# Attention in 64x64 quadrants of TensorE, with the work of two pairs of heads spread over three visits

## The chip, the cores and the metric

One core of a Trainium2 chip runs the whole kernel. The metric is device microseconds (us) of one execution, taken as the median of several executions. TensorE does the matmuls, ScalarE the exponentials, logarithms and sines, VectorE and GpSimd the elementwise work. PSUM, where TensorE writes, is used by this kernel as four "bank pairs" of 2 x 512 float32 per partition.

## The reference

Normalised queries and keys, softmax attention, then two products with an activation between them:

```python
q_n, k_n = rmsnorm(q, g_q), rmsnorm(k, g_k)          # q, k, v: 8 x 12 x 448 x 64
attn = softmax(q_n @ k_n.T / sqrt(64))
x = (attn @ v).transpose(0, 2, 1, 3).reshape(3584, 768)
h = x @ w_in                                          # w_in: 768 x 2048   "first product"
g = h + sin(alpha * h)**2 / (alpha + 1e-9)
out = g @ w_out                                       # w_out: 2048 x 768  "second product"
```

The kernel leaves out the softmax's maximum. It gets the sums of the exponentials by a second matmul against ones beside each value matmul, and multiplies by exp(-ln(sum)).

## The kernel before

A batch has 12 heads, taken as six pairs. Keys come in tiles: three of 128 tokens for one pair, and a rest of 64 tokens that is computed for two pairs at once. So three shapes of the TensorE array alternate: scores in 64\*128 (contraction over 64, 128 outputs), values in 128\*64, the rest in 64\*64.

```python
psum = ctx.enter_context(tc.tile_pool(name="ps", bufs=4, space=bass.MemoryType.PSUM))

def scores(pi, t, warm=0):                     # pair pi, key tile t of 128: mode 64*128
    sc = bank_pair("sc")
    ...
    for hi in range(2):
        r = slice(hi * 64, hi * 64 + 64)
        nc.tensor.matmul(sc[:, hi, :S], kt[r, t * P:(t + 1) * P], qt[r, :], start=True, stop=True)
    nc.scalar.activation(expT[pi][:, 2 * t:2 * t + 2, :], sc[:, :, :S], ACT.Exp, scale=SCALE)

def attend(pi):                                # values and sums: modes 128*64 and 64*64
    av = bank_pair("av")
    for t in range(NT + 1):
        for part in range(2):
            for hi in range(2):
                ...
                nc.tensor.matmul(av[o, part, :S], lhsT, rhs, start=(t == 0), stop=(t == NT))
    rec = rpool.tile([P, S], F32, tag="rec", name="rec")
    nc.scalar.activation(rec, av[:, 1, :S], ACT.Ln)
    nc.scalar.activation(rec, rec, ACT.Exp, scale=-1.0)
    ...
    for hi in range(2):
        nc.vector.tensor_mul(xT[b][r, hp, :], av[r, 0, :S], rec[o, :])
```

A bank pair `av` comes free only after ScalarE's logarithm, ScalarE's exponential, and both VectorE products.

Steps of the previous batch's second product are the fillers. They keep TensorE busy while ScalarE makes exponentials. Each pair of heads is one visit:

```python
for p in range(NP):                            # NP = 6 pairs; for each batch b >= 1
    ...
    scores(pi, 0)
    scores(pi, 1)
    if p:
        attend(pi - 1)
    ...
    if p % 2 == 0:
        rest_scores(pi)                        # 64*64, for pairs pi and pi + 1
    scores(pi, 2)
    beside_e(4 * p)                            # norm of later batches, loads
    fill(...)                                  # some 9 steps of the second product (128*128)
    ...
attend(b * NP + NP - 1)
first_product(b, beside_h(b))
```

Of the kernel before, what the change touches and what calls it, by code (L numbers as in the profile page):

```python
# [32 lines left out]
def kernel(  # L33
# [19 lines left out]

    nc = tc.nc
# [9 lines left out]
    NJ = S // REST  # L64
    NC = NP // 2
    SCALE = float(D) ** -0.5
    HALF = D_MODEL // 2
    BUSY = (20, 8, 0, 8, 4, 4, 4, 4)
# [10 lines left out]
    epool = ctx.enter_context(tc.tile_pool(name="expT", bufs=3))  # L79
# [7 lines left out]
    def bank_pair(name):  # L87
        return psum.tile([P, 2, 512], F32, tag="ps", name=name)
# [11 lines left out]
    def rest_rows(pi, hi):  # L100

        r = (hi + pi) % 2
        return slice(r * 64, r * 64 + 64)

    def load_v(b):


        vb[b] = vpool.tile([P, NT * H + NP, D], BF16, tag="vb", name="vb")
        parts = []
        tok = v[b].rearrange("h (p j) d -> p h (j d)", j=NJ)  # L110
        for jj in range(2):
            parts.append((vb[b][jj * 64:jj * 64 + 64, :NT * H, :].rearrange("p (h t) d -> p h (t d)", t=NT),
                          tok[:, :, jj * NT * D:(jj + 1) * NT * D]))
        last = v[b].rearrange("(hi dp pp) (p j) d -> j hi pp p dp d", hi=2, pp=2, j=NJ)[NJ - 1]
        slots = vb[b][:, NT * H:, :].rearrange("p (dp pp) d -> pp p dp d", pp=2)
        for hi in range(2):
            for pp in range(2):
                parts.append((slots[pp][rest_rows(pp, hi)], last[hi, pp]))
        return [lambda o=o, i=i: nc.gpsimd.dma_start(out=o, in_=i) for o, i in parts]  # L119
# [64 lines left out]
    def norm_tasks(ci):  # L184
# [3 lines left out]

# [29 lines left out]
        def scale(w):  # L218
            eng = nc.vector if early else nc.gpsimd
            if st.n is None:  # L220
                st.n = npool.tile([P, 2, NJ, 2, D], BF16, tag="qkn", name="qkn")
            n, x = st.n[:, w], qk[ci][:, w].rearrange("p (hi j) d -> p hi j d", hi=2)
            inv = st.inv[w].rearrange("p (hi j) -> p hi j", hi=2)
            for hi in range(2):
                if w == 0:
                    eng.tensor_mul(n[:, :, hi, :], x[:, hi], inv[:, hi].unsqueeze(2).to_broadcast([P, NJ, D]))  # L226
                else:
                    eng.tensor_mul(  # L228
                        n[:, :2 * NT, hi, :].rearrange("p (t jj) d -> p jj t d", jj=2),
                        x[:, hi, :2 * NT].rearrange("p (jj t) d -> p jj t d", jj=2),  # L230
                        inv[:, hi, :2 * NT].rearrange("p (jj t) -> p jj t", jj=2).unsqueeze(3).to_broadcast([P, 2, NT, D]))
            if w == 1:
                eng.tensor_mul(n[:, NJ - 1], x[:, :, NJ - 1], inv[:, :, NJ - 1].unsqueeze(2).to_broadcast([P, 2, D]))
# [33 lines left out]
    def scores(pi, t, warm=0):  # L267

        sc = bank_pair("sc")
        for _ in range(warm):  # L270
            nc.tensor.matmul(sc[:, 0], blank[:, :P], blank, start=True, stop=True)
        qt, kt = qkT[pi][:, 0, :], qkT[pi][:, 1, :]
        if pi not in expT:
            expT[pi] = epool.tile([P, 2 * NT + 1, S], BF16, tag="expT", name="expT")
        for hi in range(2):
            r = slice(hi * 64, hi * 64 + 64)
            nc.tensor.matmul(sc[:, hi, :S], kt[r, t * P:(t + 1) * P], qt[r, :], start=True, stop=True)  # L277
        nc.scalar.activation(expT[pi][:, 2 * t:2 * t + 2, :], sc[:, :, :S], ACT.Exp, scale=SCALE)  # L278

    def rest_scores(pi):  # L280

        sc = bank_pair("sc3")
        for pp in range(2):
            if pi + pp not in expT:
                expT[pi + pp] = epool.tile([P, 2 * NT + 1, S], BF16, tag="expT", name="expT")
            for hi in range(2):
                r = slice(hi * 64, hi * 64 + 64)
                nc.tensor.matmul(sc[rest_rows(pp, hi), pp, :S], qkT[pi + pp][r, 1, NT * P:S], qkT[pi + pp][r, 0, :],  # L288
                                 start=True, stop=True)
        for pp in range(2):  # L290
            nc.scalar.activation(expT[pi + pp][:, 2 * NT, :], sc[:, pp, :S], ACT.Exp, scale=SCALE)  # L291

    def attend(pi):
# [3 lines left out]
        e = expT[pi]  # L297
        av = bank_pair("av")
        for t in range(NT + 1):
            for part in range(2):  # L300
                for hi in range(2):
                    o = slice((hi + part) % 2 * 64, (hi + part) % 2 * 64 + 64)
                    if t < NT:
                        lhsT = ones if part else vb[b][:, (hi * NP + hp) * NT + t, :]
                        rhs = e[:, 2 * t + hi, :]
                    else:
                        r = rest_rows(pi, hi)
                        lhsT = ones[r, :] if part else vb[b][r, NT * H + hp, :]
                        rhs = e[r, 2 * NT, :]
                    nc.tensor.matmul(av[o, part, :S], lhsT, rhs, start=(t == 0), stop=(t == NT))  # L310
# [23 lines left out]
    def first_product(b, beside):  # L334
# [11 lines left out]
        for i in range(EARLY):  # L346
            tiles[i] = bank_pair("hps")
            for m in (2 * i, 2 * i + 1):
                mm(tiles[i], m, range(KT - 1))
        for i in range(MT // 2):  # L350
            if i >= EARLY:
                tiles[i] = bank_pair("hps")
            for m in (2 * i, 2 * i + 1):
                mm(tiles[i], m, [KT - 1] if i < EARLY else range(KT))
            for m in (2 * i, 2 * i + 1):
                late.append(snake(b, tiles[i][:, m % 2, :S], m))
                if len(late) > 1:
                    late.popleft()()
            for task in beside.get(i, ()):
                task()  # L360
# [77 lines left out]
    def step_of(ci, *steps):  # L438
        return lambda: [norm[ci].steps[n]() for n in steps]
# [9 lines left out]
    FIRST, KEPT = 16, MT // 2  # L449
    for p in range(NP):  # L450
        scores(p, 0, BUSY[2 + p])
        scores(p, 1)
        if p:
            attend(p - 1)
        if p == 0:
            c1.rsqrt()
        if p % 2 == 0:
            rest_scores(p)
        scores(p, 2)
        if p == 0:  # L460
            c2.square(0), c2.square(1)
            c2.fold_g()
            c1.scale(0), c1.scale(1)
            c2.reduce(0), c2.reduce(1)
            load_qk(NC)
        if p == 1:
            c1.pe_transpose((0, 1))
            c2.rsqrt()
            c2.scale(0), c2.scale(1)
            load_qk(NC + 1)  # L470
            load_w_out(0)
            begin_norm(NC)
            step_of(NC, 0, 1, 2)()
        if p == 2:
            c2.pe_transpose((0, 1))
            step_of(NC, 3, 4)()
            v_parts = load_v(1)
            v_parts[0](), v_parts[1]()
            begin_norm(NC + 1)
            step_of(NC + 1, 0, 1, 2)()  # L480
        if p == 3:
            step_of(NC, 5, 6)()
            step_of(NC + 1, 3, 4)()
            for part in v_parts[2:]:
                part()
            load_w_out(1)
        if p == 5:
            step_of(NC + 1, 5)()
    step_of(NC + 1, 6)()
    attend(NP - 1)  # L490
    first_product(0, beside_h(0))

    for b in range(1, B):
# [20 lines left out]
        def beside_e(slot):  # L514
            for task in at[slot]:
                task()

        for p in range(NP):
            pi = b * NP + p
            if p == 0:  # L520
                quota = min(FIRST, n_fill)
            else:
                left = max(n_fill - FIRST, 0)
                quota = left * p // (NP - 1) - left * (p - 1) // (NP - 1)
            part = [quota * j // 4 for j in range(5)]
            if p == 0 and b > 1:
                fill(part[2])
            scores(pi, 0)
            scores(pi, 1)
            if p:  # L530
                attend(pi - 1)
            else:
                fill(part[3] - (part[2] if b > 1 else 0))
            if p % 2 == 0:
                rest_scores(pi)
            scores(pi, 2)
            beside_e(4 * p)
            if p:
                fill(part[2])
                beside_e(4 * p + 1)  # L540
                fill(part[3] - part[2])
            else:
                beside_e(4 * p + 1)
            beside_e(4 * p + 2)
            fill(part[4] - part[3])
            beside_e(4 * p + 3)
        attend(b * NP + NP - 1)
        for slot in range(4 * NP, len(at)):
            beside_e(slot)
# [31 lines left out]
```

## Time and profile before

| | before |
|---|---|
| time, median of 4 runs | 457.88 us (457.71 to 459.25) |
| TensorE busy | 96% of the span |
| one batch (first product to first product, batches 2 to 7) | 52.47 us |
| ... its 271 matmul slots at their own pace | 48.27 us |
| ... its 33 changes of array mode | 3.70 us |
| ... the rest, which is waits | 0.50 us |
| first product of batch 0 starts | 46.6 us |

The last four lines come from the start of every matmul in the trace. A slot is one matmul, or two or four that run side by side in parts of the array. It takes 189 ns for 448 columns and 162 ns for 384. What a start is late by, where the shape of the array changes, is booked as a mode change, and what is left as a wait. The split is sharper than the waits that the profile lists, because a listed wait counts only from the modelled end of the group before.

The profile's own list of TensorE's waits (columns: total us, times, longest) has these two on top for the whole run:

```profile
PE av L310 <- ACT expT L278: 3.0, 9, 0.9
PE av L310 <- DMA vb<-in_v_dram: 2.2, 1, 2.2
```

The second is one wait of batch 0 for V. No value or score waits for VectorE's product `xT`.

### The profile page before, as it was taken

Reading aid. Unit: us, or ns where it says so; the run is one execution under the profiler, and the core shown is the slowest. Engines: PE = TensorE matmul, PEld = TensorE weight load, DVE = VectorE, ACT = ScalarE, POOL = GpSimd, SP = SyncE. Lnnn points to the kernel's source line nnn. Section 1 sums busy time; section 2 is a strip of 40 time slices with the busy share of each in tenths; the row PEclk is TensorE's granted clock in tenths of the full one; section 3 lists DMA queues with packets and bytes.
Section 4 is the critical chain, followed back from the end, with each engine's and each line's share of the span. In section 5 each row is a group of like instructions: output and inputs, shape, how many; then the busy total and the mean of one; then the engine's idle time right before and its main releaser. Section 6 shows DMA issues by size and latency. Waiting matters only on the chain.

```text
span 456.9 us, 7795 instructions
## 1 busy us (share of the span) xinstructions
PE 436.8 (96%) x2952; PEld 215.0 (47%) x2956; DVE 227.9 (50%) x334; ACT 341.6 (75%) x555; POOL 293.1 (64%) x299
## 2 busy tenths in 40 slices
PE   7678999999999999999999999999999999999996
PEld 3333544445444554445444554445544454445563
DVE  3774374536545465444655364554745364333621
ACT  4869788868888688877888589777888588876700
POOL 3977977777768687686668697686677686002400
PEclk9989999999999999999999999999999999999999
DMA  6999999378055922579064941469043750410022
GB/s 242 185 243 243 219 159 245 94 148 153 2 156 156 142 93 69 113 161 204 0 156 148 98 145 30 128 169 219 1 144 87 69 85 3 97 48 19 0 58 81
DMA packets 81833, 54.98 MB, mean 120 GB/s; under 512 B 60148, under 2 KB 78340, under 8 KB 81796
## 3 DMA queue, kind: packets, MB, share of 16 engines
q1 hardware_dynamic: 56690, 40.97, 35.1%
q0 software_dynamic: 24160, 11.81, 21.1%
q10 hardware_dynamic: 946, 1.70, 1.0%
q8 instruction: 23, 0.38, 0.3%
q14 instruction: 14, 0.11, 0.1%
HBM read 45.62 MB, written 11.01 MB: 124 GB/s over the span
## 4 chain that ended last, share of the span: by engine, by line
PE 81%; ACT 8%; issue 3%; DMA 3%; DVE 2%; POOL 2%; SPq 0%; DVEq 0%; POOLq 0%
PE hps L341 32%; PE ops L383 26%; PE av L310 16%; PE sc L277 6%; ACT expT L278 4%; DMA vb<-in_v_dram 2%; ACT expT L291 2%; DVE ms L208 1%; POOL s L325 1%; DMA g_rows<-in_g_q_dram 1%; ACT rec L313 1%; ACT rec L312 1%; PE sc L288 1%; ACT inv L215 1%; DVE g_sb L330 0%
## 5 line engine op out<-in xcount | busy, mean ns | idle before, releaser
L383 PE MATMUL ops<-w_out_sb,g_sb 128*128 128x384 bf16 x896 | 155.6, 327 | 1.9 <-DVE g_sb L330 1.0
L341 PE MATMUL hps<-xT,w_in_sb 128*128 128x448 bf16 x768 | 146.7, 353 | 0.0
L278 ACT ACTIVATE expT<-sc 128x896 bf16<-128x896 f32 x144 | 125.6, 916 | 25.5 <-PE sc L277 25.3
L383 PEld LDWEIGHTS <-g_sb 128*128 128x128 bf16 x896 | 83.6, 98 | 65.3 <-issue 13.1
L330 DVE SCALAR_TENSOR_TENSOR g_sb<-s,inv_alpha_sb,hps 128x448 bf16<-128x448 f32 x128 | 81.2, 676 | 63.3 <-POOL s L325 63.3
L325 POOL TENSOR_TENSOR s<-s 128x448 f32<-128x448 f32 x64 | 59.3, 930 | 76.1 <-ACT s L322 64.2
L318 DVE TENSOR_TENSOR xT<-av,rec 64x448 bf16<-64x448 f32 x96 | 59.7, 622 | 96.5 <-ACT rec L313 94.6
L341 PEld LDWEIGHTS <-w_in_sb 128*128 128x128 bf16 x768 | 74.5, 98 | 70.3 <-issue 1.6
L322 ACT ACTIVATE s<-hps,alpha_sb 128x448 f32<-128x448 f32 x128 | 74.5, 627 | 28.5 <-PE hps L341 26.8
L310 PE MATMUL av<-expT,vb 128*64 128x448 bf16 (+1 forms) x384 | 71.2, 364 | 5.2 <-ACT expT L278 3.0
L202 POOL TENSOR_TENSOR sq<-qk 128x896 f32<-128x896 f32 x42 | 69.9, 1678 | 5.9 <-DVE ms L208 3.2
L226 POOL TENSOR_TENSOR qkn<-qk,inv 128x448 bf16<-128x448 f32 x42 | 38.5, 937 | 50.4 <-issue 33.2
L310 PE MATMUL av<-expT,ones 128*64 128x448 bf16 (+1 forms) x384 | 67.1, 358 | 0.0
L205 POOL TENSOR_TENSOR qk<-qk,gg 128x896 f32<-128x896 f32 x24 | 50.1, 2090 | 3.7 <-ACT gg L155 3.3
L388 DVE COPY osb<-ops 128x768 f32<-128x768 f32 (+1 forms) x35 | 27.9, 797 | 45.5 <-PE ops L383 45.4
L208 DVE TENSOR_REDUCE ms<-sq 128x14 f32<-128x896 f32 x42 | 44.8, 1081 | 9.8 <-POOL sq L202 9.6
L277 PE MATMUL sc<-qkT 64*128 64x448 bf16 x288 | 44.7, 359 | 2.0 <-ACT expT L291 0.6
L310 PEld LDWEIGHTS <-vb 128*64 128x64 bf16 (+1 forms) x384 | 22.8, 108 | 46.5 <-issue 39.4
L312 ACT ACTIVATE rec<-av 128x448 f32<-128x448 f32 x48 | 26.1, 544 | 21.7 <-PE av L310 19.5
L327 ACT ACTIVATE s<-s 128x448 f32<-128x448 f32 x64 | 36.9, 577 | 2.9
L228 POOL TENSOR_TENSOR qkn<-qk,inv 128x384 bf16<-128x384 f32 x42 | 33.9, 828 | 0.0
L119 POOL DMA_DIRECT2D vb<-in_v_dram x48 | 32.1, 686 | 0.0
(50 smaller groups left out, 196.2 us busy)
## 6 DMA issues: line engine op xcount, KB each, us to landing
qk<-in_q_dram SPq DMA_DIRECT2D x24, 448.0 KB, 5.6
qk<-in_k_dram SPq DMA_DIRECT2D x22, 448.0 KB, 7.7
out_dram<-osb SPq DMA_DIRECT2D x39, 192.0 KB, 4.7
vb<-in_v_dram POOLq DMA_DIRECT2D x16, 288.0 KB, 8.1
w_in_sb<-in_moe_w_in_dram POOLq DMA_DIRECT2D x2, 1536.0 KB, 17.5
w_out_sb<-in_moe_w_out_dram POOLq DMA_DIRECT2D x2, 1536.0 KB, 28.6
out_dram<-osb SPq DMA_DIRECT2D x26, 96.0 KB, 5.0
qk<-in_k_dram ACTq DMA_DIRECT2D x2, 448.0 KB, 6.0
```

Of the source, the lines that this page charges most:

```text
L202: nc.gpsimd.tensor_mul(st.sq[w], qk[ci][:, w], qk[ci][:, w])
L205: eng.tensor_mul(qk[ci][:, 0], qk[ci][:, 0], gg.to_broadcast([P, 2 * NJ, D]))
L208: nc.vector.reduce_sum(st.ms[:, w, :], st.sq[w], axis=AX.X)
L277: nc.tensor.matmul(sc[:, hi, :S], kt[r, t * P:(t + 1) * P], qt[r, :], start=True, stop=True)
L278: nc.scalar.activation(expT[pi][:, 2 * t:2 * t + 2, :], sc[:, :, :S], ACT.Exp, scale=SCALE)
L310: nc.tensor.matmul(av[o, part, :S], lhsT, rhs, start=(t == 0), stop=(t == NT))
L318: nc.vector.tensor_mul(xT[b][r, hp, :], av[r, 0, :S], rec[o, :])
L322: nc.scalar.activation(s1, hps, ACT.Sin, scale=alpha_sb[:, m, :])
L325: nc.gpsimd.tensor_mul(s2, s1, s1)
L330: nc.vector.scalar_tensor_tensor(g_sb[:, m, (b % 2) * S:(b % 2 + 1) * S], s2, inv_alpha_sb[:, m, :], hps, op0=ALU.mult, op1=ALU.add)
L341: nc.tensor.matmul(ps[:, m % 2, :S], w_in_sb[:, kt, m * P:(m + 1) * P], x[:, kt, :], start=(kt == 0), stop=(kt == KT - 1))
L383: nc.tensor.matmul(st["ps"][:, k, :HALF], lhsT, w_out_sb[:, m, half * HALF:(half + 1) * HALF], start=(m == 0), stop=(m == MT - 1))
```

## The change

The intent is to get rid of mode changes and the odd rest. Every key tile becomes 64 tokens wide, for two heads of two pairs at once, so all of attention runs in the 64\*64 mode. Seven such tiles per two pairs are spread over three visits; two of these visits also hold the values of one pair each, from the group of two pairs before. Cut to its core:

```diff
-    def scores(pi, t, warm=0):
+    def scores(c, j, warm=0):
         sc = bank_pair("sc")
         ...
+        for pp in range(2):
+            for hi in range(2):
+                qkt, r = qkT[2 * c + pp], slice(hi * 64, hi * 64 + 64)
+                nc.tensor.matmul(sc[key_rows(pp, hi), pp, :S], qkt[r, 1, j * REST:(j + 1) * REST], qkt[r, 0, :],
+                                 start=True, stop=True)
...
     def attend(pi):
-        for t in range(NT + 1):
+        for j in range(NJ):                        # 7 tiles of 64, all quadrants
...
     first_product: (order of its first matmuls)
-            for m in (2 * i, 2 * i + 1):
-                mm(tiles[i], m, range(KT - 1))
+        for kts in (range(KT - 2), [KT - 2], [KT - 1]):
+            ...
-    FIRST, KEPT = 16, MT // 2
+    FIRST, KEPT = 12, MT // 2
...
+    visits = [(c, *x) for c in range(NC) for x in (((0, 1), 0), ((2, 3), 1), ((4, 5, 6), None))]
...
-        for p in range(NP):
-            ...
+        for n, (c, tiles, pp) in enumerate(visits):
+            for j in tiles:
+                scores(b * NC + c, j)
+            if n == 0:
+                fill(FIRST - (FIRST // 2 if b > 1 else 0))
+            elif c and pp is not None:
+                attend(b * NP + 2 * c - 2 + pp)
+            beside_e(n, 0)
+            left = n_fill - FIRST
+            fill(left * (n + 1) // len(visits) - left * n // len(visits))
+            beside_e(n, 1)
+        attend(b * NP + NP - 2)
         attend(b * NP + NP - 1)
```

Nine visits a batch, with about five fillers each, take the place of six with about nine each. Batch 0, which has no fillers, is also reordered, and V is loaded in another layout.

## The prediction

> **What bounds the kernel now.** I read the page's head and its slices, then the chain that ended last, then TensorE in order of time over one batch, then ScalarE and VectorE beside it.
>
> ```profile
> span 456.9 us, 7795 instructions
> PE 436.8 (96%) x2952; PEld 215.0 (47%) x2956; DVE 227.9 (50%) x334; ACT 341.6 (75%) x555; POOL 293.1 (64%) x299
> ...
> PE 81%; ACT 8%; issue 3%; DMA 3%; DVE 2%; POOL 2%; SPq 0%; DVEq 0%; POOLq 0%
> ```
>
> TensorE is busy 96% of the span and holds 81% of the chain; the clock row stands at 9 throughout. So time is gained or lost only on TensorE, by fewer or shorter gaps there. The windows of two stretches of one batch (each batch but the first repeats them; columns: length, then busy PE, PEld, DVE, ACT, POOL, clock, DMA) (the second product of the batch before and attention; then the first product):
>
> ```profile
> 221.73:256.03 34.30, 33.96 (x257) 16.27 (x255) 17.44 (x23) 27.60 (x44) 25.67 (x27) 1.00 0.42 109
> 256.03:274.20 18.17, 18.17 (x100) 9.41 (x97) 9.69 (x15) 14.30 (x24) 12.81 (x13) 1.00 0.82 138
> ```
>
> A batch is 52.47 us, of which 34.30 is the stretch that the change touches (TensorE idle 0.34 of it, though the busy column counts the tails of overlapping matmuls too). Within it, TensorE and its neighbours in order of time:
>
> ```profile
> 233.86 0.55 PE L277 MATMUL sc<-qkT 64*128 64x448 bf16 x4
> 234.35 0.38 PE L310 MATMUL av<-expT,vb 128*64 128x448 bf16 x2
> 234.56 0.36 PE L310 MATMUL av<-expT,ones 128*64 128x448 bf16 x2
> 234.75 0.36 PE L310 MATMUL av<-expT,vb 128*64 128x448 bf16 x2
> ...
> 235.32 0.35 PE L310 MATMUL av<-expT,ones 128*64 128x448 bf16 x2
> 235.60 0.38 PE L310 MATMUL av<-expT,vb 64*64 64x448 bf16 x2
> 235.61 0.38 PE L310 MATMUL av<-expT,ones 64*64 64x448 bf16 x2
> 235.81 0.36 PE L288 MATMUL sc<-qkT 64*64 64x448 bf16 x4
> 236.11 0.36 PE L277 MATMUL sc<-qkT 64*128 64x448 bf16 x2
> 236.40 2.77 PE L383 MATMUL ops<-w_out_sb,g_sb 128*128 128x384 bf16 x16
> ```
>
> The first column is the start. Two 128*64 matmuls run at once and the next two start 0.19 later; four 64*64 matmuls also start together and take one slot. But 235.32 to 235.60 is 0.28, and 235.81 to 236.11 is 0.30: where the shape of the array changes, about 0.1 is lost. The evacuation of a finished `av`:
>
> ```profile
> 230.55 0.38 PE L310 MATMUL av<-expT,ones 64*64 64x448 bf16 x2
> ...
> 230.98 0.54 ACT L312 ACTIVATE rec<-av 128x448 f32<-128x448 f32 x1
> ...
> 231.56 0.58 ACT L313 ACTIVATE rec<-rec 128x448 f32<-128x448 f32 x1
> 232.04 0.90 ACT L278 ACTIVATE expT<-sc 128x896 bf16<-128x896 f32 x1
> 232.16 1.26 DVE L318 TENSOR_TENSOR xT<-av,rec 64x448 bf16<-64x448 f32 x2 [2.59 <-ACT rec L313]
> ```
>
> The last group starts at 230.54, its bank pair is free at 233.42: 2.88 later. Today this hides, as one `av` comes every 5.1 to 5.25 us.
>
> **What the Trainium skill says.** "TensorEngine Tiling (Array Packing)", Key Properties: changing the tiling mode drains the engine, changing the tile does not. The trace agrees: reading all matmul starts, a change of mode adds 93 to 103 ns to the start of the first group and 10 (after 64*128 or 128*128) to 24 ns (after 128*64 or 64*64) to the second. "TensorE: Matmul & The Clock Gate", on the warm gap: N/2.4 + 2.5 ns, 189 for 448 columns; the trace has 189 within a mode, also for quadrants. The tiling page's "PSUM Bottleneck" says that tiling speeds TensorE, not the emptying of PSUM: here that is the 2.88 us above, and the change leaves it as it is. "ScalarE: Activation LUTs", What ACT_TABLE_LOAD costs: ACTIVATEs back to back overlap by about 93 ns; the trace has 0.92 for one 128x896 exponential and 1.73 for two.
>
> **The change part by part.**
> *Matmul slots.* Per two pairs of heads, before: 6 score slots, 1 for the rest, 2 x 7 for values = 21. After: 7 + 2 x 7 = 21. Nothing is gained here; 63 slots a batch x 0.1895 = 11.94 us in both. 56 second-product steps (112 x 0.162 = 18.14) are the same.
> *Mode changes.* Before, a pair with values: full to 64*128 (108 ns), 128*64 (117), 64*64 (121), 64*128 (114), full (107) = 567; five such a batch, 554 for the first pair and 352 for the last values: 3.74 us in 33 changes. After: nine visits and the last values, each full to 64*64 (118) and back (114): 20 changes, 2.32. Saved: 1.42 a batch. 11.94 + 18.14 + 3.74 = 33.82 against 34.30, so 0.48 waits before.
> *Exponentials.* Per two pairs 6 x 0.82 + 0.87 = 5.8 becomes 7 x 0.82 = 5.7: nothing, and ScalarE isn't the bound.
> *PSUM.* Four bank pairs; one is always held by the second product's accumulation, so three rotate. The changed program, built but not run, names what each instruction waits for. From the second group of heads on: the second visit's `av` takes the pair of the first visit's `av` and waits for its VectorE product; the third visit's middle scores take that pair again, and wait likewise; its last scores take the pair of its own first scores, and wait for their exponential.
> Visit timeline (first scores at 0): second scores 0.21, values from 0.40, their last group 1.56, end 1.74, mode 0.10, five steps 1.63, mode 0.09: next visit at 3.57. Exponentials end at 0.41 + 1.73 = 2.14, so Ln starts there (PE alone would allow 2.0), bank free at 2.14 + 2.44 + 0.05 = 4.63. The next values want it at 3.97: wait 0.66. In the third visit the middle scores come 3.4 after the start of those values, and the bank 4.09 after: wait 0.7. The last scores can start 0.41 + 0.92 + 0.06 = 1.39 after the first ones, where the middle ones end at 1.10: wait 0.29. Together 1.65. For the second group of heads the first of these is 0.5, but its first values wait 0.2 for an exponential of the third visit before; for the first group there are no values, and I find no wait. Per batch 1.7 + 1.65 = 3.35.
> *Sum of a batch.* 32.4 + 3.35 = 35.75 against 34.30: +1.4. Seven batches: +10. (Batch 1 has only four steps in a visit, so longer waits, but also fewer before its values; I take it as the rest.)
> *Start.* Batch 0 has no second product. First values come only after nine score tiles, so the 2.2 us in which TensorE waits for V at 20.7 vanish, and the second group's keys are copied out of PSUM ahead of a 2.08 us reduction. Following ScalarE's queue from its first exponential at 14.35 (7 exponentials, 1.8 of squares, then 14 exponentials, six times 1.13, and four short norm steps, with some 2.5 of idle for transposes and values) the last values start near 43.5 and the first product at 45.1, where it was 46.7: -1.5.
> *First product.* Same 96 x 189 ns; its order gives 16, then 4 matmuls before the last two pairs are needed: 3.0 and 3.8 us against 2.6 of evacuation. No wait.
> Sum: 457.8 + 9.8 - 1.5 = 466.
>
> **Rivals.** (1) The mode changes are all that counts and the bank waits fall away (for example as ScalarE and VectorE are quicker in turn than I chained them): 7 x (-1.42 - 0.48) - 1.5 = 443. For it: the tuned counts of warm-ups and fillers. Against: the waits are in the program by name, and 2.88 us of evacuation is measured. (2) Half of the waits: 454. (3) Quadrants in a row can't keep 189 ns: four weight loads and four matmuls a slot, which before never had more than two slots in a row. At 200 ns, 54 x 0.011 x 7 = +4: 470. Against: the two in a row at 235.60 and 235.81 lie 0.21 apart, as any first two after a change. (4) Batch 0 shortens by 4 instead of 1.5: 463.
>
> **Range and chances.** The centre is 466 by the sum; rivals 2 and 4 pull more than 3, so I say 465, with 456 to 471. The 2% lines are 448.7 and 467.0: faster 0.05, same 0.58, slower 0.37.
>
> **What would show it.** All attention matmuls 64*64 at slots of 0.19; two mode changes a visit; in the list of waits of TensorE, new entries of values and scores waiting for VectorE's `xT` product and for exponentials, some 3 us a batch, 0.3 to 0.7 each; a batch of 53.9; the first product of batch 0 at about 45. A list of waits still near empty, or batches of 51, would make me wrong.

## The result, and the profile after

| | before | the change |
|---|---|---|
| median (range), 4 runs each | 457.88 (457.71 to 459.25) | 469.57 (468.47 to 470.00) |
| ratio, 95% interval | | 1.0245 (1.0219 to 1.0271): slower |
| one batch | 52.47 | 54.06 |
| slots / mode changes / waits | 48.27 / 3.70 (33) / 0.50 | 48.27 / 2.27 (20) / 3.52 |
| first product of batch 0 starts | 46.62 | 45.59 |

Ratios here and below are the mean of one kernel's runs over that of the other's of the same rounds, so they are not quite the ratio of the medians quoted. Executions over 1.5% slower than the fastest of the same kernel are left out of the means.

From the page of the changed kernel: the head, the chain that ended last by engine, and the two groups of attention matmuls.

```profile
span 466.7 us, 9464 instructions
...
PE 433.9 (93%) x3815; PEld 220.3 (47%) x3820; DVE 227.5 (49%) x331; ACT 342.8 (73%) x531; POOL 278.2 (60%) x262
...
PE 66%; ACT 16%; DMA 6%; DVE 5%; issue 4%; POOL 2%; SPq 1%; DVEq 0%; POOLq 0%
...
L277 PE MATMUL av<-expT,vb 64*64 64x448 bf16 x672 | 71.8, 353 | 9.6 <-DVE xT L286 6.4
...
L262 PE MATMUL sc<-qkT 64*64 64x448 bf16 x672 | 53.2, 365 | 10.1 <-DVE xT L286 7.3
```

TensorE's share fell from 96% to 93%, and its share of the chain from 81% to 66%, while ScalarE's and VectorE's shares there grew. TensorE does not have less slot work than before (48.27 us a batch in both); it waits more. Both groups name VectorE's product as what ended most of their idle time. The list of TensorE's waits over the whole run confirms it:

```profile
PE sc L262 <- DVE xT L286: 7.3, 14, 0.6
PE av L277 <- DVE xT L286: 6.4, 14, 0.7
PE av L277 <- ACT expT L265: 3.0, 5, 1.1
```

Fourteen of each is two per batch in seven batches. The wait for V is gone from the list. In order of time, in the second and third visit of the last group of heads of a batch (start, length, engine, line, ...):

```profile
193.43 0.35 PE L277 MATMUL av<-expT,vb 64*64 64x448 bf16 x2
...
194.86 1.80 PE L353 MATMUL ops<-w_out_sb,g_sb 128*128 128x384 bf16 x10
...
196.27 1.26 DVE L286 TENSOR_TENSOR xT<-av,rec 64x448 bf16<-64x448 f32 x2 [2.69 <-ACT rec L281]
196.59 0.57 PE L262 MATMUL sc<-qkT 64*64 64x448 bf16 x8
197.58 0.38 PE L277 MATMUL av<-expT,vb 64*64 64x448 bf16 x2 [0.42 <-DVE xT L286]
...
200.34 1.26 DVE L286 TENSOR_TENSOR xT<-av,rec 64x448 bf16<-64x448 f32 x2 [2.81 <-ACT rec L281]
200.76 0.38 PE L262 MATMUL sc<-qkT 64*64 64x448 bf16 x4
201.65 0.90 PE L262 MATMUL sc<-qkT 64*64 64x448 bf16 x8 [0.50 <-DVE xT L286]
```

The first `av` starts at 193.43, and its products end at 196.27 + 1.26 = 197.53, which is 4.10 later. The next visit's first scores start at 196.59, so its values could start 0.40 later, at 196.99. They start at 197.58, right after that product: 0.59 lost. The bracket says 0.42, because it counts from the modelled end of the score matmuls. The same happens in the third visit. Its middle scores could start at 200.97 and start at 201.65, just after the next product ends at 201.60: 0.68 lost. Its last scores then wait for an exponential: eight matmuls take 0.90 there, against 0.57 in the visit above, so 0.33.

The gap is thus the price of a rhythm. A bank pair is held for about 4.1 us, and the program asks for it again after about 3.5. Before, one `av` came every 5.1 to 5.25 us.

### The profile page after: what moved, and what is told of

It reads as the page before. It is cut to its first block, busy times and chain, and to the rows that moved or that the text cites. A ratio compares the mean times of both kernels' runs of the same rounds, so it can differ in the third digit from the quotient of the medians.

```text
span 466.7 us, 9464 instructions
## 1 busy us (share of the span) xinstructions
PE 433.9 (93%) x3815; PEld 220.3 (47%) x3820; DVE 227.5 (49%) x331; ACT 342.8 (73%) x531; POOL 278.2 (60%) x262
## 4 chain that ended last, share of the span: by engine, by line
PE 66%; ACT 16%; DMA 6%; DVE 5%; issue 4%; POOL 2%; SPq 1%; DVEq 0%; POOLq 0%
PE hps L309 27%; PE ops L353 25%; ACT expT L265 11%; PE av L277 9%; PE sc L262 5%; DVE xT L286 4%; DMA qkT<-qkn 3%; ACT rec L281 2%; ACT rec L280 2%; DMA out_dram<-osb 1%; DMA g_rows<-in_g_q_dram 1%; POOL qkn L220 1%; SPq L226 1%; POOL qk L200 1%; SPq L102 1%
## 5 line engine op out<-in xcount | busy, mean ns | idle before, releaser
L265 ACT ACTIVATE expT<-sc 128x896 bf16<-128x896 f32 x168 | 144.0, 914 | 33.8 <-PE sc L262 33.7
L353 PE MATMUL ops<-w_out_sb,g_sb 128*128 128x384 bf16 x896 | 157.8, 327 | 0.0
L353 PEld LDWEIGHTS <-g_sb 128*128 128x128 bf16 x896 | 82.4, 98 | 70.6 <-issue 20.3
L220 POOL TENSOR_TENSOR qkn<-qk,inv 128x448 bf16<-128x448 f32 x84 | 76.1, 937 | 38.2 <-issue 21.0
L277 PE MATMUL av<-expT,vb 64*64 64x448 bf16 x672 | 71.8, 353 | 9.6 <-DVE xT L286 6.4
L277 PE MATMUL av<-expT,ones 64*64 64x448 bf16 x672 | 71.7, 353 | 0.0
L262 PE MATMUL sc<-qkT 64*64 64x448 bf16 x672 | 53.2, 365 | 10.1 <-DVE xT L286 7.3
L277 PEld LDWEIGHTS <-vb 64*64 64x64 bf16 x672 | 38.2, 107 | 34.4 <-issue 15.0
L203 DVE TENSOR_REDUCE ms<-sq 128x14 f32<-128x896 f32 x42 | 45.1, 1081 | 17.2 <-POOL sq L197 16.6
L277 PEld LDWEIGHTS <-ones 64*64 64x64 bf16 x672 | 34.8, 107 | 4.2
L262 PEld LDWEIGHTS <-qkT 64*64 64x64 bf16 x672 | 15.4, 104 | 43.2 <-issue 29.1
```

The source lines that it names most:

```text
L220: eng.tensor_mul(n[:, :, hi, :], x[:, hi], inv[:, hi].unsqueeze(2).to_broadcast([P, NJ, D]))
L262: nc.tensor.matmul(sc[key_rows(pp, hi), pp, :S], qkt[r, 1, j * REST:(j + 1) * REST], qkt[r, 0, :], start=True, stop=True)
L265: nc.scalar.activation(expT[c, j], sc[:, :, :S], ACT.Exp, scale=SCALE)
L277: nc.tensor.matmul(av[o, part, :S], ones[r, :] if part else vb[b][r, hp, j, :], expT[pi // 2, j][r, pi % 2, :], start=(j == 0), stop=(j == ...
L353: nc.tensor.matmul(st["ps"][:, k, :HALF], lhsT, w_out_sb[:, m, half * HALF:(half + 1) * HALF], start=(m == 0), stop=(m == MT - 1))
```

## The experiments

My theory: the quadrants themselves save time by fewer mode changes; the three visits cost more than that, because an `av` is asked back before ScalarE and VectorE have emptied it. The rival theories: the quadrants themselves are slower (their pace, or their four weight loads a slot), or ScalarE's and VectorE's new positions relative to the norm work are at fault.

Several kernels were run once only. The state of such a run is unknown, but all their clocks were 0.99 to 1.00, and I judge them by their batch in the trace. The batch repeats well: 54.06 in both profiles of the change, 52.47 to 52.48 in both of the kernel before, 51.14 in both of the kernel called two_visits. "Before" ran beside them at 458.26, 458.65 and 458.99 (the third on another chip, where two_visits has the same batch).

| kernel | time us (runs) | batch us | mode changes | waits |
|---|---|---|---|---|
| before | 457.88 (4) | 52.47 | 33: 3.70 | 0.50 |
| the change | 469.57 (4) | 54.06 | 20: 2.27 | 3.52 |
| two_visits | 449.03 (4) | 51.14 | 16: 1.82 | 1.05 |
| old_three | 473.75 (1) | 54.80 | 34: 3.83 | 2.69 |
| no_rec (wrong) | 450.66 (1) | 51.45 | 20: 2.27 | 0.91 |
| two_visits_split | 453.71 (1) | 51.69 | 26: 2.95 | 0.47 |
| two_after_three | 477.30 (6) | 55.4 to 56.7 (last: 52.2) | 16: 1.82 | 5.30 |
| uneven | 467.89 (1) | 53.93 | 20: 2.27 | 3.39 |
| two_three_tasks | 459.45 (6) | 52.58 | 16: 1.82 | 2.49 |
| two_three_fill | 455.43 (6) | 51.94 | 16: 1.82 | 1.85 |

Changes and waits are of the same batch of each trace; for two_after_three that batch took 55.38.

### two_visits: quadrants kept, two visits per two pairs

```diff
-    visits = [(c, *x) for c in range(NC) for x in (((0, 1), 0), ((2, 3), 1), ((4, 5, 6), None))]
+    visits = [(c, *x) for c in range(NC) for x in (((0, 1), (2, 3), 0), ((4, 5), (6,), 1))]
...
+            for j in later:                        # after the values, before the fillers
+                scores(b * NC + c, j)
```

> All attention in quadrants as in the change, batch 0 as in the change, but from batch 1 on two visits per two pairs (tiles 0 and 1, values, tiles 2 and 3; then 4 and 5, values, 6), which is the order that the kernel before had. Theory (the three visits cause the waits on PSUM, quadrants themselves only save mode changes): 14 mode changes a batch in place of 33, 1.62 us in place of 3.74; values now 4.5 us apart against 4.09 to empty the bank pair, so the waits on VectorE's product vanish; left are 0.3 for each fourth score tile and 0.3 for one values visit, some 0.9. Batch 32.6 + 18.2 = 50.8 us (before 52.5, the change 54.1), time about 446, faster than both. Rival (quadrants are slow in themselves, or four matmuls a slot starve the queue): batch stays at 53 to 54, time 462 to 470.

It took 449.03 us (448.69 to 449.80). The ratio to before is 0.9792 (0.9770 to 0.9814), which is faster. The batch is 51.14, where I had expected 50.8. The 16 mode changes are two more than I had counted, since the first visit's later scores come after fillers; the waits are 1.05 in place of 0.9. The stretch of second product and attention, in the columns of the windows above, for the change and for two_visits:

```profile
225.16:261.05 35.89, 33.77 (x365) 16.93 (x364) 16.22 (x22) 27.81 (x41) 25.21 (x24) 1.00 0.52 122
```

```profile
217.43:250.40 32.97, 32.62 (x365) 17.48 (x364) 16.31 (x22) 27.09 (x41) 25.21 (x24) 1.00 0.50 128
```

The same 365 matmuls take 2.92 us less, and ScalarE, VectorE and GpSimd do the same work (41, 22 and 24 instructions). In order of time:

```profile
228.28 0.57 PE L262 MATMUL sc<-qkT 64*64 64x448 bf16 x8
...
228.68 0.35 PE L277 MATMUL av<-expT,vb 64*64 64x448 bf16 x2
...
230.00 0.87 PE L262 MATMUL sc<-qkT 64*64 64x448 bf16 x8
...
231.51 1.26 DVE L286 TENSOR_TENSOR xT<-av,rec 64x448 bf16<-64x448 f32 x2 [1.71 <-ACT rec L281]
...
233.51 0.57 PE L262 MATMUL sc<-qkT 64*64 64x448 bf16 x8
```

The `av` of 228.68 is free at 232.77, after 4.09 us: the emptying is as slow as in the change. But the next visit starts 5.23 us after this one (228.28 to 233.51), so the emptying lies behind work. This says that the quadrants are not slow, and that the order in three visits is. The norm work isn't what differs: between 180 and 400 us, ScalarE's waits for the norm's reduction are the same four, 1.5 us together, in the kernel before, the change, two_visits and old_three.

### old_three: the old shapes in three visits

```diff
-        for p in range(NP):
-            ... (scores 0 and 1, attend, rest, scores 2, fill)
+        for n, (c, part) in enumerate(visits):     # nine visits
+            pi = b * NP + 2 * c
+            if part == 0:   scores(pi, 0); scores(pi, 1)
+            elif part == 1: scores(pi, 2); rest_scores(pi)
+            else:           scores(pi + 1, 0); scores(pi + 1, 1); scores(pi + 1, 2)
+            ...
+            elif c and part < 2:
+                attend(pi - 2 + part)
```

It also has the change's order of the first product, FIRST = 12 and a fourth buffer for exponentials.

> The other half alone: the shapes of before (64*128, 128*64, a quadrant remainder) in the three visits of the change from batch 1 on, with its filler counts and its first product; batch 0 as before. Its program waits for the same bank pairs as the change. Theory: waits as in the change (about 3.3 a batch), 34 mode changes at 3.85 us: batch 18.2 + 11.94 + 18.14 + 3.85 + 3.3 = 55.4 us. Rival (quadrants cause the loss): batch near 52.5 as before.

It took 473.75 us in its one run; its batch is 54.80, where I had expected 55.4 (I had put the waits at 3.3, and they are 2.69). The same waits appear without one quadrant tile of the new kind:

```profile
253.95 0.38 PE L310 MATMUL av<-expT,vb 128*64 128x448 bf16 x2 [0.21 <-DVE xT L318]
...
257.25 0.36 PE L277 MATMUL sc<-qkT 64*128 64x448 bf16 x2
258.13 0.85 PE L277 MATMUL sc<-qkT 64*128 64x448 bf16 x4 [0.52 <-DVE xT L318]
```

The last two starts lie 0.88 apart in one mode, where a slot is 0.19: 0.69 lost to VectorE's product, as in the change. With this run the change splits into two steps, order and shapes (us per batch):

| | old shapes | quadrants | quadrants' effect |
|---|---|---|---|
| one visit per pair | 52.47 | 51.14 | -1.33 |
| three visits per two pairs | 54.80 | 54.06 | -0.74 |
| three visits' effect | +2.33 | +2.92 | |

The step called order is not the visits alone: old_three and two_visits both also have the change's order of the first product, FIRST = 12, values of the group before, and another spread of the norm work over the batch. None of these was run by itself. They are not what the change loses by, since two_visits has them too and is faster than before; but the -1.33 and the +2.33 include them. The cleaner measure of the three visits is the +2.92, between two kernels that differ in the visits and in what is dealt evenly over them.

The saving in mode changes is about the same in both rows (3.70 to 1.82, and 3.83 to 2.27). In the three visits half of it is given back as waits (2.69 to 3.52): the values that waited 0.28 in old_three wait 0.57 to 0.59 in the change, since TensorE arrives earlier at a bank pair that comes free no sooner.

### no_rec: the emptying made shorter, with a wrong result

```diff
-        rec = rpool.tile([P, S], F32, tag="rec", name="rec")
-        nc.scalar.activation(rec, av[:, 1, :S], ACT.Ln)
-        nc.scalar.activation(rec, rec, ACT.Exp, scale=-1.0)
+        rec = ones_wide                            # a constant: the result is wrong, and meant to be
```

> The change with the reciprocal's Ln and Exp left out (values multiplied by a constant 0.0001, so the result is wrong on purpose): the bank pair of values is free 2.9 us after they start in place of 4.09, below the 3.57 of a visit. The pool of bank pairs then also gives the last tile of the third visit another pair. Theory: all waits of a batch but a small one vanish, batch 54.06 - 3.4 = 50.7 us. Rival (fillers, quadrant pace or mode changes cost more than counted): batch stays above 52.5.

The order of the change stands. But the bank pairs are dealt otherwise, as the expectation says, and ScalarE loses work too: it is busy for 23.44 us of the stretch of second product and attention, 27.81 in the change. The batch fell from 54.06 to 51.45. The four waits for VectorE's product (0.57, 0.67, 0.59 and 0.67, together 2.50) are gone. Of what is left, 0.91, one wait of 0.20 is for values, and two of 0.30 are before the third visits' last scores:

```profile
235.39 0.96 DVE L358 COPY osb<-ops 128x768 f32<-128x768 f32 x1
235.70 1.08 PE L264 MATMUL sc<-qkT 64*64 64x448 bf16 x12
236.13 1.73 ACT L267 ACTIVATE expT<-sc 128x896 bf16<-128x896 f32 x2 [1.83 <-PE sc L264]
```

The last four of these twelve matmuls start at 236.40, while the first of the two exponentials still runs, so they no longer wait for it as they do in the change. They wait for VectorE's copy `osb` of the second product's result, which ends at 236.35. These 0.6 are most of the 0.75 by which my expectation of 50.7 was too low. So 2.5 of the 3.5 us go with Ln and Exp, and not with the number of matmuls or the mode. Whether a lighter ScalarE helps in them beside the shorter emptying, this run alone doesn't separate; two_visits and old_three leave ScalarE its work, and there the waits go and stay with the order. The total was 450.66 us.

### two_visits_split: fewer waits, or fewer mode changes

```diff
+            fill(quota // 2)
             for j in later:                        # moved into the middle of the fillers
                 scores(b * NC + c, j)
+            fill(quota - quota // 2)
```

> two_visits with the scores after the values moved into the middle of the fillers: 12 more mode changes a batch at 0.116 us = 1.39, less the 0.5 to 0.6 of waiting for the exponential that the move hides. Theory: batch 0.8 to 1.4 us longer than two_visits. Rival (a mode change costs nothing, the drain is hidden): the same or shorter.

The batch is 51.69 against 51.14 of two_visits: 0.55 longer, where I had expected 0.8 to 1.4 and twelve more mode changes. By the starts, ten more mode changes cost 1.13, or 0.11 each as elsewhere, while waits fell by 0.58, from 1.05 to 0.47. The batch shows the difference of the two; the price of a change is still read from the starts. The rival, that a mode change costs nothing, falls, since the batch grew although the waits fell. two_visits already sits on the right side of that trade.

### two_after_three, two_three_tasks, two_three_fill: trying to shorten two_visits

In two_visits the first group of heads has no values yet, and its two visits hold seven tiles. I thought that three short visits for that group alone would remove the exponential waits there.

```diff
+    two = (((0, 1), (2, 3), 0), ((4, 5), (6,), 1))
+    three = (((0, 1), (), None), ((2, 3), (), None), ((4, 5, 6), (), None))
+    visits = [(c, *x) for c in range(NC) for x in (two if c else three)]
```

> two_visits, but the first group of heads of a batch, which has no values beside it, keeps the three visits of the change. Its fourth score tile then no longer waits 0.26 us for an exponential; mode changes stay 16. Theory: batch 51.14 - 0.26 = 50.9 us, 1.8 us less in all, time about 447. Rival: shorter filler stretches (6.3 steps in place of 7.3) bring the wait of values for VectorE's product back, batch 51.1 or more.

This missed by far: 477.30 us, ratio 1.0401 (1.0369 to 1.0433). The norm tasks of later batches are dealt evenly over the visits; with seven visits instead of six they came at other places relative to the work. ScalarE, in order, stands at a logarithm of the norm whose input VectorE has not reduced yet, and all exponentials stand behind it. The list of ScalarE's waits over the whole run:

```profile
ACT inv L210 <- DVE ms L203: 21.4, 21, 2.6
```

TensorE then waits 2.2 us in one go for an exponential. In three of batches 2 to 6 more is lost: 0.5 to 1.9 us after this wait the granted clock is half for some 3.4 us (0.51 and 0.50 in the windows 145.3 to 148.7 and 203.3 to 206.7), and matmuls of the second product start 0.32 us apart there in place of 0.16. These three batches take 56.4 to 56.7; the two without such a stretch take 55.4. In the change, batches 1 to 7 run at full clock.

To test that, the next kernel puts the tasks where they were relative to the work, and the last deals the fillers so that visits with values have more.

```diff
+            bounds = (0, 3, 5, 8, 12, 16, 20, 24)                     # two_three_tasks
+            a, z = bounds[v], bounds[v + 1]
...
+            cut = [left * x // 44 for x in (0, 5, 10, 16, 23, 30, 37, 44)]   # two_three_fill, with bounds too
+            fill(cut[n + 1] - cut[n])
```

> two_after_three with the norm's tasks for later batches put back to the places in time that they have in two_visits (a table of bounds in place of an even split over seven visits). Theory (two_after_three lost because ScalarE's Ln of the norm came before VectorE's reductions were done, 2.6 us of waiting in one go): that wait vanishes, batch 50.9 us. Rival (the shorter filler stretches or the order of visits is at fault): batch stays above 52.

> two_three_tasks with the fillers cut 5, 5, 6, then 7 in each visit with values, in place of an even 6.3: values 0.2 us further apart. Theory: same mode changes, batch 50.8 to 50.9 us, at most 0.2 shorter than two_three_tasks; rival: nothing to tell from two_three_tasks.

The first took 459.45 us, ratio 1.0016 (0.9992 to 1.0040), with a batch of 52.58. The wait of ScalarE for the reduction shrank to 0.4 us in a batch, as in two_visits, so the place of the tasks was indeed the cause of most of the miss. What remains was there in two_after_three already, though not in two_visits: in the first group, the second product waits for an exponential (0.87 in both), and values wait for `osb`, the copy of the second product's result (0.48, now 0.61). The second took 455.43 us, ratio 0.9919 (0.9898 to 0.9939), batch 51.94: better, but still 0.8 above two_visits, 0.61 of it being values that wait for the copy `osb`. Between 180 and 400 us of the span the profile lists it first among TensorE's waits:

```profile
PE av L277 <- DVE osb L358: 1.7, 4, 0.4
```

I had expected 50.8 to 50.9 of all three. The waits for exponentials in the first group, at which the idea aimed, did not go: 0.26 in two_visits, 0.30 and 0.87 in two_three_tasks. Dealing the fillers otherwise took most of the 0.87 away.

### uneven: the change with its fillers dealt otherwise

```diff
-            fill(left * (n + 1) // len(visits) - left * n // len(visits))
+            cut = [left * x // 44 for x in (0, 4, 9, 14, 21, 28, 29, 36, 43, 44)]
+            fill(cut[n + 1] - cut[n])              # visits with values get 7, the third visits 1
```

> The change with its three visits, but the fillers moved: 7 steps in the two visits with values, 1 in the third (5 each before). Values are then 4.2 us apart, as long as it takes to empty their bank pair, so the waits for VectorE's product should go; but the third visit is only 1.1 us and its three exponentials take 2.6, so the next scores and values wait for those, about 1.5 us in the middle of a batch and 0.6 at its end. Theory: waits 2.3 to 2.5 in place of 3.5, batch about 53.0 us. Rival (the waits are from the sheer number of visits or changes): batch stays at 54.1.

I expected 53.0, and the batch is 53.93, hardly below the change's 54.06. The waits for VectorE's product did go, as expected: between 180 and 400 us the list has none. But others came, 3.39 in all where I had expected 2.3 to 2.5:

```profile
241.34 0.38 PE L277 MATMUL av<-expT,vb 64*64 64x448 bf16 x2 [0.61 <-DVE osb L358]
...
247.38 0.38 PE L262 MATMUL sc<-qkT 64*64 64x448 bf16 x4 [0.42 <-ACT expT L265]
...
248.19 0.38 PE L277 MATMUL av<-expT,vb 64*64 64x448 bf16 x2 [0.43 <-ACT expT L265]
```

With one filler in a third visit, values now wait for that visit's exponentials, and in another place for the copy `osb`. Dealing the same fillers otherwise, in this one way at least, does not mend three visits.

### The change, the kernel before and two_visits once more

No edit; these runs show how firm the start of batch 0 is.

> The change once more, to see how its start scatters: batches of 54.06 us as in the first profile; the first product of batch 0, at 45.6 in the first profile, may move by 1 us, as kernels with the same batch 0 had it between 44.6 and 46.9.

> The kernel before once more: batches of 52.47 us; the first product of batch 0 at 45.3 to 46.6. If the two starts overlap, the 1.5 us that I predicted to be gained there can't be told from scatter.

> two_visits once more on the same chip as the two above: batch 51.14 us, time 449, 2.1% faster than before; its start may move by 1 us.

The change took 470.63 us and before 459.34 in one run each; two_visits 449.35 (448.71 to 450.06), ratio 0.9791 (0.9770 to 0.9813). The batches came out the same as the first time. The start did not. The first product of batch 0 started at 45.59 and 47.20 in the change, and at 46.62 and 46.91 before. Over nine traces with the change's batch 0 (no_rec left out) it starts from 45.4 to 47.2, 46.14 on average; over three with the old one, from 45.3 to 46.9, 46.28 on average. The granted clock goes with this scatter. In the windows of the change and of the change again (clock is the third number from the end):

```profile
14.30:17.70 3.40, 3.20 (x26) 0.95 (x25) 2.49 (x4) 2.64 (x5) 3.40 (x6) 1.00 1.02 244
32.00:35.40 3.40, 3.35 (x27) 0.97 (x30) 3.00 (x4) 2.06 (x4) 1.31 (x1) 0.61 1.06 246
```

```profile
14.30:17.70 3.40, 3.40 (x17) 0.87 (x16) 2.50 (x5) 1.83 (x3) 3.40 (x6) 0.50 1.06 256
32.00:35.40 3.40, 2.56 (x43) 1.40 (x43) 2.91 (x5) 1.57 (x3) 0.00 (x0) 1.00 1.06 244
```

Batch 0 of all these traces but one has a stretch at half clock. In five of the nine with the change's batch 0 it lies near 32 to 36 us, and the start is 45.4 to 45.6; in three it lies near 11 to 18 us, and the start is 46.9 to 47.2; in one near 20 to 24 us, with 46.5. With the old batch 0, the trace without one starts at 45.3, that with one near 30 to 34 us at 46.6, and that with two at 46.9. Why the stretch falls here or there with one and the same program, no run here settles.

## Why the prediction was right or wrong

The time on record was 465 with a range of 456 to 471; 469.57 lies in it. The likeliest class, "within 2%", was narrowly wrong: the ratio is 1.0245, and "slower" had been given 0.37. Point by point:

- **Slots: right.** 48.27 us of slots per batch in both kernels. In rows of quadrants a slot is 189 ns, the median of over 200 gaps; the four matmuls of a slot start 3 ns apart. Rival 3, 200 ns a slot, falls.
- **Mode changes: right.** 20 a batch; 2.27 us against 2.32 said. The saving is 1.43 against 1.42.
- **Bank waits: right, each by name and nearly by size.** Said: 0.2 for the first values, 0.5 or 0.66 for the second values, 0.7 for the third visit's middle scores, 0.29 for its last ones, 3.35 a batch. Measured: 0.20; 0.57 and 0.59; 0.67 and 0.67; 0.33 and 0.33: 3.36 by this list, and 3.52 with small ones. That these waits are the cause, and not only present, is shown by no_rec (shorter emptying, waits gone), two_visits (another order, these waits gone) and old_three (other shapes, same waits). Rivals 1 and 2, no waits or half of them, fall.
- **The batch: 0.14 short.** The stretch of second product and attention was said to become 35.75 us; the windows have 35.89. Of the 0.14, the waits are +0.17 and the changes -0.05. From 34.30, which the prediction shows, that is +1.59 a batch, where +1.4 was carried on into the sum: 1.1 us over six batches.
- **Batch 1: right enough.** Taken as the rest, +1.4; measured +1.3 in the first pair of profiles and +1.9 in the second.
- **The start: this is the term that was mis-sized.** "First product at 45.1, where it was 46.7: -1.5." The wait of 2.2 us for V did vanish, as said, but only about -0.1 is left on average (46.14 against 46.28), lost in the scatter of the start. I had read one trace of the kernel before as if its start were firm to 0.1 us. I had also misread its page: the clock row does not stand "at 9 throughout", its third slice is an 8, and that is the stretch at half clock in batch 0 (30.5 to 33.9 us). Where that stretch lies late in both kernels, the start is 46.6 before and 45.4 to 45.6 after, a gain of 1.0 to 1.2; in three of the change's nine traces it lies early, and the gain is gone. Rival 4, a start shorter by 4, falls too.

The accounts close. In the first profiles: -1.03 for the start, +1.28 for batch 1, six times 1.59 for the others, together 9.79, and the spans differ by 466.7 - 456.9 = 9.8. In the second profiles: +0.29 + 1.86 + 9.54 = 11.7, and the spans differ by 468.9 - 457.2 = 11.7. The medians differ by 11.7 as well.

Taking 1 us off the sum of 466 "because two rivals pull more" moved it away from the result. None of those rivals had evidence as strong as the waits that the built program names. The share of 0.58 for "within 2%" followed from a centre 2 us below its line, 467.0, with the -1.5 of the start in it. Without the start's gain the same sum is 457.8 + 9.8 = 467.6, just beyond that line.

So the time came within the range with 1.4 us to spare, and not by errors that cancel: nearly every one of them pulled the sum down.

What stays open is what places the half-clock stretches of batch 0, and with them the start, and whether an order of visits beats two_visits; four attempts did not. Of all kernels that ran here, two_visits is the fastest with a right result: 2.1% below before and 4.4% below the change (449.03 against 469.57).

## What to carry to other kernels

Before splitting work into more and shorter visits, compare two times: how long a visit's PSUM buffer is held until its last reader is done, and how long until the program asks for that buffer again. Here it is held for 4.1 us; asked back after 5.2 it costs nothing, after 3.5 it costs 0.6 each time, and saving TensorE's time just ahead of such a wait only lengthens the wait. When a change has two parts, such as shapes and order, run each alone: here one part (with the small changes that came with it) was worth -1.3 us a batch and the other +2.9, and together they looked like one bad idea.

## What the Trainium skill lacked or had wrong

- "TensorEngine Tiling (Array Packing)", Key Properties, says that a change of mode drains TensorE, but gives no time. Here a change adds 93 to 103 ns to the first group after it and 11 to 24 ns to the second; with ten more changes, 1.13 us more of a batch went to mode changes.
- "TensorEngine Tiling (Array Packing)", PSUM Bottleneck, warns that emptying PSUM may become the limit and advises both ScalarE and VectorE. It does not say that a chain of the two holds the buffer for the sum of their times: here logarithm, exponential and two products end 4.1 us after the first value matmul, and asked back after 3.5 us they cost 2.5 us a batch in waits of 0.57 to 0.67.
- I found no page that gives the pace of rows of 64x64 quadrants, from one group of four to the next: 189 ns per four matmuls of 448 columns here, with four weight loads of 107 ns each in a slot that stay hidden.
